# Splitting a channel transform by even and odd samples, with its sums on GpSimd, in a fused attention and spectral-filter kernel

## The chip, the cores and the metric

One core of one Trainium2 chip runs the whole program. The metric is the device time of one execution in microseconds (us), as the median of several executions. Engine names are those of the profile: PE is TensorE, DVE is VectorE, ACT is ScalarE, POOL is GpSimd and SP is SyncE, which starts most of the DMAs.

## What is computed

```
x: (1, 2048, 448) bf16      16 heads of 28 channels
g = sigmoid((x * gate_w).sum(-1))
a = softmax(q k^T * 28**-0.5) v @ wo            q, k, v = x @ wqkv
b = irfft2(rfft2(x) * (w_r + 1j * w_i))         over the 2048 rows and the 448 channels
out = g * a + (1 - g) * b
```

All inputs and the output are bf16.

## The kernel before

**Attention.** The 16 heads stand in 4 groups of 4, a head in each strip of 32 partitions. The queries are cut into 4 chunks of 512 and the keys into 16 tiles of 128. That makes 16 pairs of a group and a chunk, taken one after the other, with 16 key tiles each: 256 blocks, where a block is the scores of 4 heads, 128 keys and 512 queries. A block goes one of two ways.

- On the ACT way, two heads are one step: two matmuls write a two-bank PSUM tile (`psA` and `psB` in turn), and one exponential of 1024 columns writes two slots of `ring`, a ring of 28 slots in SBUF. Four matmuls per block then add `vw` times `ring` into the PSUM bank `pvb`.
- On the DVE way, an exponential is approximated. One matmul per head (in the plan: `dunit`) writes a single PSUM bank (`bg`), and one DVE clamp (line 991, 512 columns) makes a 16-bit pattern in a tile `pd` from it. Three `int64_add` on POOL (line 1001) make three shifted copies, each into another of the 9 `pd` tiles, and four times four matmuls with differently scaled values `vd` add all four into `pvb`.

The list `ND` says how many of the 16 key tiles of each pair go the DVE way. Its sum is 73, so 183 blocks, or 366 exponentials, go to ACT.

**The spectral part**, called the background, is done by matmuls with constant matrices, spread between the attention work. `fwd` transforms the channels of one of 16 token tiles: four chunks of 128, 128, 128 and 65 input channels against `Bd`, 450 output columns each (225 cosines and 225 sines), copied to `X1`. `fwd2` multiplies by `A`, is copied to `Ab`, and a DMA spreads it over `xtok`. `mid`, for 16 values of g, multiplies by `CS` (450, 225 and 225 columns), forms two products with the weights `Wg`, subtracts and adds these into `Z` on DVE, and multiplies `Z` by `CS` again (450, 225, 225). `inv` collects rows by a DMA into `V2`, multiplies by `A` and scales by the gate into `zt`. `out_tile` and `last_tile` add four matmuls of `zt` with `Binv` (448 columns) to four of the attention's result with the padded `wo`, and scale by the gate into the output.

**The order** of everything is fixed when the program is written. Each operation is put on a list, and a long packed number table, `TABLE`, says in which order the list is emitted and which PSUM bank each item of the background gets. Each engine then works through its own instructions in that order and waits at each for the semaphores that it needs. An engine that waits holds back all that stands behind it.

**GpSimd's code.** Before an instruction of another kind, the built program of this kernel holds a row `ISA` without a tile on POOL, which puts another library of code into GpSimd. `int64_add` stands in one library and `tensor_tensor` in another; memsets, copies and casts need neither. In the order below, `ISA pd<-pd` is an `int64_add`, and a bare `ISA` is such a change of library. The program before has one, ahead of its first `int64_add`.

Of the kernel before, what the change touches and what calls it, by code (L numbers as in the profile page):

```python
# [13 lines left out]
BF16 = mybir.dt.bfloat16  # L14
# [8 lines left out]
F2 = 2 * F  # L23
NT, J, P = 16, 8, 128
FS, FN = (0, 112), 113
# [6 lines left out]
NPD, DKT = 9, 5  # L32
FILL0 = 60000
DUE_P = 4.0
TABLE = (
    "eNoN1oNyHloUQOF9tI//NGmjKqlt27Zt27Zt27Zt27Zt+95nWDPfLA1VAIBALAiFMGgAbSAcIiASPMSGOBAX4kF8iAID0dABEkBCSASJIQkk"
    "hWSggIKEFMAgAAhpIQTSgICaYKEGdIRsUB1SQUpIDtUgHaSHypAFUoOD7JADMkEGyAnBkBEyQ1YoBjEhBlSEXFAcSkApKA1BkB9KQm7IA4td"
    "GegNVaEcVIKy0ALyQj4oDF2gAMQk5aEg1IEKUAiKwBIXi4SSp1AUnkEYCScRpAdEktjkObyAl/AKXsMbiENyYC6MS+KRtxCfRJGcGE0SkIQk"
    "EXkHK2AlrILVsAbWQmKyDtZDT0hCJsBEmASTIQ/egSmwAWpDbtwId+Ee3IdNsBm2wFbYBtthB0yD6ZAXH8AMmAmzYDbMgbkwDx5CQ9jmdkJd"
    "mA8cFkAt2AULYREshkewBJZCE3gM+bAARrvd0BSewDJoBvlxDyyHvbAP3kNLSEoK4gf4CI1hP3SFA/AJPkM3KIKF8CDUhx1uKrSFwpiMJCeH"  # L40
    "oDmE6S9QFA9DCnIEjkJKUgyPwVcI1cXxG0wnM0gqMhBmkuNQCltDCUxNTkBJ7AxVSTUyi6Qh1UlprEHSklbQCU5CGUxH0pOyWJNkIBlJJlIO"
    "T8FpOANn4RychwtwEcrjbFIBs5Ih0B4yk2wkO8lBcpJc5DvkJpfgMuQhFTEvScAqYT6y012Bq5CfJGTXYLO7DgVIQVKIVMYbcBOykFtwG6pg"
    "YVKElCFVsSgpS4qRavgDfkJx8guSsepYAyN1claO1MTy5DdUILUwWtfGcB2b1cHYOg4bTerBH6iL9bAXJGIVyRiSmI0l3aE+jiOLXBLWAIEQ"
    "QgkjDXE84aQRCIJEEkU0aYTtIIIZ8g8sScoi2V9wxJPGGCBRLiULIk0wBqlEgklc3RTj62YYxkJICZJUN8d6rgVWJqVJfVeFtMSSpIFL58JZ"
    "K0zFGrrWmN41cnFZCtYGM7h4LLnO6NpiatYOM7lolky3x4Q6DUvPOmBCV4rUIolcYtcRM7BOGJ+lZUlcOtYZE+kumJEldVG6K8bR3bAwy8Qi"
    "dGLdA7tjEVacRbFcLIlOoXthT8zBEujemJul1CVYPJ2TZWF5WCqdl2VmfbAe6Yv1STbWD1Pr7KwBaUj6YyNSlBVjAzCrzqIHYkE2CAdjMZeV"
    "FXfZdCE2BEu42iSNHoql2DCsQwqwzDqHHo4lXSVWkpVyI7AuyalHYhFdhlVm5Vg+VpblZ6MwrS7N8uvRmFuPwfIsl07mxmJ1Ng6TuxRuPKZ0"
    "FdgEzKcL6YpsIg6CSZjKZdDpdTVWg2XXRfVknIKNSV3WjOXVefRULKanYQFdlU3Heqwzqc1mYBfSlczEOmwWdiNldEfWnczGOTgXm7PCuqCu"
    "yWqxediJldLNyXxsQRZgCV1aN2ELsSmrwhZhS9KKLMYl2IK1JvVZS1ZOl9QNWW63FNuyZdiOLcfiuqxegeV1PpdOr8T8rhHL41ZhLd2YFXAZ"
    "9Wos6Aq5NdiZdWFtWAW9FnuS+nod9mC9SD29HjfgUteEZNIbsQHrySrq3qSS3oR9yGasrWvoLdjMbcW+pClp7rZhe9bCdWD9SEO9HZuRlm4H"  # L50
    "9mOtXFPdn3VjO7GOHsx2YWvWWFfVNfVu3IN92BDWQu/F5ro768v2YWXdi/VmbUk7sh8P4EjWnoxiHchBbKlHQ0cylB3Cuno8tGKHsZw7gsNY"
    "XjecjWDlXQV3FHuQiu4YjmOdSCXXSY9lx7GBPoFDSRN9EgeyUziBTWSt9Wkcz7rqRrqLHkZSuzTuDJ7DtC6bG07O4giS3Y0kg1gOl9OdxwuY"
    "y61gK1l73ZVNJAPYJVzGLuJy1k5fxklkFWtDruBksppNIcPgKo5m1XQzPZWMYTPZNWylr2M3PYlNYTewg57FJrOp7Cb2J7ewmruNHXUbPYHM"
    "Z2NgALmDbfVdnM6quxlsAbuHS9hSVsPdx866pnuA3fVisoQsJcvIQ5zNlpNa7hH20EP1AD2NDNOD9BMcRR7jXDaHbWVVtGdj9Rj9FLexZ7ib"
    "bHF7yF6yj9wjz/E+eUAekmnsEZlD9pMD5CB5TJ6Qp+QQ6amfkcPkCHlOjpJjZAh5QQaRZe44mccC7AQ5SU6RV3iavMCXOFAvZCP1XDKPrCKL"
    "yGoyn6wga8hL8oqsJevIa1xPXpMNZCPZRHrpN6S6foNvyWayhWwl28hb3E52kJ3kHS4gi9l69o5M0EP0B9zMNrD3uIsMJMP1YP0Rt7A17BOu"
    "Y3tYZfcZp+sqbrT+govYATZO72UT9VdcyxaSwWQj+4bj3Cj9Hfvpg2y828T66Ml6gvuBp9lJdortZL/wDPuJQWy8HqEnuml6kvuN8/Qf3MeG"
    "ub84S//DXWw/286Gu91shAOZ2fUBIrO4wo7KHWyKzuqYPM4m6SLuBBvpRjkuhSzqrrC5+iqbqlHeZVJeYDP0RXaYHWFztJKz9T12iGlpZHxa"
    "2pVxvbWVR1kULetmaierOi9DWDQ9xubrleQsS0ADMiYLku1cQrpAx5DnWXtX29VxwfI+6+AesMEQIju6mPIS6+TW6FhyhV6pr7FQeYacJefI"
    "eRIm++rL7AK5SC6RyyRc3mbX2Tl2hVwl18gtdoddJzfITRIhb5HbJFLeIf3cKn2XxJY7dRy5UH8ii3R/956s13Flf/2KLdOvWTy51T1kA9xA"  # L60
    "FyUXuvhyg37Etuho2c19IAnkGzbIbdPLXUK53a3VS3UM9pEkki9Yd/eEvWQ3WA+XWPZ0SWRSeVC/Zb3cOv2ZJZPP2HO2Wm/VyWVd94WlkE/Z"
    "V7ZDT3Mp5WM23X1jN9kflkru0qnlDPeXpZGMz3Scz3KbdDqZVn5k79lm3dnt1enlUOjiMshP7DvbqD+wo3qJ/sEyykzyH9un37HMcrsG3tVl"
    "kYT/ZPt1Y5dVZpOGU75bW75HZ5f94Bc7pGOxHNLxnDKUHdCtXRP3m3mueC55TB/WuWWAa55HtnFBvK37TI7ovPK4jsklzye/kK8kv0ReQJ7Q"
    "sXgkD+EXdGx+TX8j30koLygLyWAexhO423q0Kywv6cR8jDupi8gRcEcXlVf1KZ2Ep+DFZAx+RV/UxWVKHs4juOAlZFM32I11l3VJGZ+Xkj9I"
    "PP5AP9ZD3GJdWkbxm7qMTMOf67IyLf9J4vKhrpyM5tf1L5KAl5cVZEL+myzXt3RFWUkm4ql4al5ZxuFJ+Sv9h1SR6fhf8lCf0VXlI93bpefV"
    "ZFZ+Qz/R1eU/0sfVkNl5X3dPJ+P3dU2ZmdeSL/RdnZzn4Nl4Jl5bznNZeB0529WVz/R8N8fVk6d1Ab7AFeSTXX2Zkc91b3QDOcXl5G/1WZ2Y"
    "NpS5eBKalE51yWgjmZxm4E1kEZ6bN5aF+GtdmL/U5zTQpzoPbyrz8WayKM/Pm0tC32lK3+vyvARvIRmtwFvKFe6DXulaSU5XudZyl1vtdjtB"
    "i/M17oduI/PytpKbdrIkF6a9LMX3uBAak8aiofSX3uv2uQ6ykwyjH/Unfdt1lP90BD2vI2kxHpvGoZ3lXx2XdpFlOTPlODVrXVfZTZbmSCUd"
    "Cftdd9lDluHrXGOu6EnXhGtqaE9ZhfeSv3Vvud590xtcH/lTV+Vf9UanjaV95QF32vWTm1xFXp834I7+0f3lKBgga/DK/K7zNIYJMwOlNDV5"
# [78 lines left out]
def fft_consts():  # L148
# [1291 lines left out]
```

## Time and profile before

| | |
|---|---|
| median of 3 runs | 384.12 us (384.02 to 384.2) |
| profiled execution | 384.64 us; its span, first to last instruction, 382.8 us |
| granted TensorE clock | 0.999 |
| PE, DVE, ACT, POOL busy, share of the span | 98%, 87%, 90%, 65% |
| exponentials, clamps, int64_adds | 366, 292, 219 |

The page gives the busy time of each engine, the costliest groups of instructions, and the chain of work that ended last. Lines are those of the kernel before. All matmuls are issued by one helper and so share line 426; tiles tell them apart. Spans on POOL are rough by the profiler's own word.

### The profile page before, as it was taken

What the parts mean: (1) busy time and instruction counts of PE and PEld (TensorE: products, weight loads), DVE (VectorE), ACT (ScalarE), POOL (GpSimd) and SP (SyncE); (2) the same over time, 40 slices, a digit from 0 to 9 for tenths busy, and PEclk for the clock granted to TensorE, in tenths of its full rate; (3) what the DMA queues carried; (4) which work ended last, traced back from release to release, by engine and by line L of the source; (5) the groups of instructions that cost most, each with busy time, mean ns of one, the idle gap of its engine ahead of it and who ended that gap; (6) DMA issues with size and microseconds to landing.
All of it is one profiled execution on the core that took longest, in us unless ns stands there. A gap on an engine that the chain in (4) does not pass through costs nothing.

```text
span 382.8 us, 12650 instructions
## 1 busy us (share of the span) xinstructions
PE 375.9 (98%) x5140; PEld 140.7 (37%) x5141; DVE 333.4 (87%) x620; ACT 346.3 (90%) x381; POOL 247.3 (65%) x276
## 2 busy tenths in 40 slices
PE   8999999999999999999999999999999999999996
PEld 5643322233423222334434434333333333333444
DVE  1778977889899999999999999999999998878623
ACT  2699999999999999998996899999999999998861
POOL 5753874475764988647575594988769656564810
PEclk9999999999999999999999999999999999999999
DMA  8421010001112232222220132221323131122111
GB/s 228 101 58 52 4 33 2 21 25 21 22 40 48 70 130 61 53 44 71 48 65 10 30 70 47 76 57 23 82 51 82 53 97 44 46 64 64 48 57 63
DMA packets 31158, 21.68 MB, mean 57 GB/s; under 512 B 16260, under 2 KB 28796, under 8 KB 31100
## 3 DMA queue, kind: packets, MB, share of 16 engines
q1 hardware_dynamic: 29708, 20.41, 20.7%
q8 instruction: 40, 0.66, 0.7%
q10 hardware_dynamic: 1392, 0.46, 0.5%
q14 instruction: 18, 0.15, 0.1%
HBM read 14.97 MB, written 1.96 MB: 44 GB/s over the span
## 4 chain that ended last, share of the span: by engine, by line
PE 77%; DVE 9%; ACT 4%; DMA 3%; issue 2%; POOL 2%; SPq 1%; ACTq 0%; POOLq 0%; DVEq 0%
PE bg L426 31%; PE pvb L426 27%; PE psA L426 9%; PE psB L426 8%; ACT ring L1032 4%; DVE pd L991 4%; POOL pd L1001 2%; DMA X<-in_A_wqkv_dram 1%; PE bg L429 1%; DMA V<-xtok 1%; SPq L401 1%; DVE vw L864 1%; DMA Rb<-rsc 1%; DVE sq L745 1%; DMA wv<-in_gate_w_dram 1%
## 5 line engine op out<-in xcount | busy, mean ns | idle before, releaser
L1001 POOL INT64_ADD pd<-pd x219 | 224.8, 1041 | 98.8 <-DVE pd L991 23.6
L1032 ACT ACTIVATE ring<-psA 128x1024 bf16<-128x1024 f32 x183 | 192.5, 1052 | 13.0 <-PE psA L426 6.0
L991 DVE TENSOR_SCALAR pd<-bg 128x512 uint16<-128x512 f32 x292 | 190.3, 684 | 14.8 <-PE bg L426 4.7
L1032 ACT ACTIVATE ring<-psB 128x1024 bf16<-128x1024 f32 x183 | 192.5, 1052 | 5.0 <-PE psB L426 3.1
L426 PE MATMUL pvb<-pd,vd 128*32 128x512 bf16 x1168 | 102.0, 384 | 0.5 <-POOL pd L1001 0.2
L426 PE MATMUL bg<-q,k 32*128 32x512 bf16 x292 | 98.3, 383 | 0.4 <-DVE vt L877 0.3
L426 PEld LDWEIGHTS <-k 32*128 32x128 bf16 x1024 | 36.8, 91 | 117.9 <-issue 113.2
L426 PE MATMUL psA<-q,k 32*128 32x512 bf16 x366 | 71.9, 384 | 0.1
L426 PE MATMUL psB<-q,k 32*128 32x512 bf16 x366 | 71.4, 383 | 0.5 <-ACT ring L1032 0.4
L426 PE MATMUL pvb<-ring,vw 128*32 128x512 bf16 x732 | 66.7, 384 | 0.1
L426 PEld LDWEIGHTS <-vd 128*32 128x32 bf16 x1168 | 27.7, 94 | 37.3 <-issue 30.6
L426 PEld LDWEIGHTS <-vw 128*32 128x32 bf16 x732 | 17.7, 95 | 22.1 <-issue 17.4
L426 PEld LDWEIGHTS <-xT 128*128 128x128 bf16 (+3 forms) x512 | 19.3, 96 | 13.3 <-issue 11.7
L426 PE MATMUL bg<-Bd,xT 128*32 128x450 bf16 (+1 forms) x256 | 19.7, 358 | 0.0
L426 PE MATMUL bg<-xT,wpq 128*32 128x512 bf16 (+2 forms) x244 | 19.2, 382 | 0.0
L426 PE MATMUL bg<-xT,wpk 128*32 128x512 bf16 (+1 forms) x240 | 19.2, 383 | 0.0
L1343 DVE TENSOR_TENSOR t<-bg,Wg 128x450 bf16<-128x450 f32 x32 | 18.9, 618 | 0.1
L426 PE MATMUL bg<-Bd,X 113*32 113x448 bf16 x224 | 16.3, 355 | 0.0
L426 PE MATMUL bg<-wvr,xT 128*128 128x112 bf16 (+1 forms) x192 | 13.0, 213 | 0.0
L426 PEld LDWEIGHTS <-CS 128*32 128x32 bf16 x384 | 9.4, 95 | 8.7 <-issue 6.0
L1388 DVE TENSOR_TENSOR X<-bg,ogb 113x512 bf16<-113x512 f32 x16 | 10.7, 686 | 1.9 <-PE bg L426 1.7
L740 DVE TENSOR_SCALAR k<-bg 128x512 bf16<-128x512 f32 x15 | 10.3, 687 | 1.2 <-PE bg L426 1.2
(115 smaller groups left out, 297.6 us busy)
## 6 DMA issues: line engine op xcount, KB each, us to landing
Rb<-rsc SPq DMA_DIRECT2D x60, 64.0 KB
CS<-cCS SPq DMA_DIRECT2D x16, 192.0 KB
Wg<-in_B_w_i_dram SPq DMA_DIRECT2D x64, 28.1 KB
xtok<-Ab SPq DMA_DIRECT2D x16, 112.5 KB
V<-xtok SPq DMA_DIRECT2D x16, 112.5 KB
xtok<-in_A_x_dram SPq DMA_DIRECT2D x3, 448.0 KB
Wg<-in_B_w_r_dram SPq DMA_DIRECT2D x32, 28.1 KB
out_dram<-wpk SPq DMA_DIRECT2D x6, 112.0 KB
```

The source lines that it names most:

```text
L401: self.pin(e.dma_start(out=out() if callable(out) else out, in_=in_() if callable(in_) else in_))
L426: self.pin(self.nc.tensor.matmul(out, lhsT=lhsT, rhs=rhs, start=start, stop=stop, **kw))
L429: self.pin(self.nc.tensor.transpose(out=out, in_=in_, identity=self.c("ident")[0:n, 0:n]))
L740: self.pin(nc.vector.tensor_scalar(out=dst, in0=self.bgi(it), scalar1=SQ, scalar2=None, op0=ALU.mult))
L745: self.pin(nc.vector.tensor_tensor(out=sqs, in0=dst, in1=dst, op=ALU.mult))
L864: self.pin(nc.vector.tensor_tensor(out=free_dims(self.vw[g][:], [[128, nv], [32, 4], [1, DH]], 4 * b * 128), in0=src, in1=wv, op=ALU.mult))
L991: self.pin(nc.vector.tensor_scalar(out=ys[:, s, :].bitcast(U16), in0=self.bgi(it), scalar1=127 * UNITS, scalar2=0.0, op0=ALU.add, op1=ALU. ...
L1001: self.pin(nc.gpsimd.int64_add(out=fl(pds), in0=fl(ys), in1=PHASE[f] * 0x0001000100010001))
L1032: self.pin(nc.scalar.activation(out=self.ring[:, u0:u0 + len(st), :], in_=slot[:, 0:len(st), :], func=ACT.Exp, scale=LN2 / UNITS))
L1343: self.pin(nc.vector.tensor_tensor(out=out[:], in0=self.bgi(it)[:, 0:F2].rearrange("p (a f) -> p a f", a=2), in1=free_dims(Wg[:], [[F, 2], ...
L1388: self.pin(nc.vector.tensor_tensor(out=free_dims(self.zt[0:FN], [[128, 4], [1, 128]], 512 * t), in0=self.bgi(it)[0:FN, :].rearrange("p (a ...
```

## The change

**The transform.** The channels are split into even and odd ones, and only 113 frequencies are computed for each half. `fwd` has the chunks of 128, 128, 96 and 97 channels, taken with a stride of two, against 226 columns instead of 450. The other frequencies follow from sums and differences of the halves: two new `tensor_tensor` on POOL for each token tile, from `X1` into one of three tiles `Xs`, which `fwd2` now reads. On the way back, two `tensor_tensor` on POOL for each g make sums and differences of `Z` into `Zs` (the first two of the `Xs` tiles), which the second product with `CS` reads; and the four matmuls with `Binv` have 224 columns instead of 448. The output is written with a stride of two.

**PSUM.** `psA`, `psB` and three single banks become three two-bank slots, `psA`, `psB` and `psC`, and one bank `bg`. The exponentials of ACT and the clamps of DVE take the slots as the table says. Items of the background take a slot's first bank or `bg`. One clamp now covers two heads (1024 columns, 154 in place of 292).

**The share.** `ND` sums to 77, so 179 blocks (358 exponentials) are left for ACT and POOL has 231 `int64_add`. `TABLE` is new.

The diff, cut to its core:

```diff
-FS, FN = (0, 112), 113
+FS, FN = (0, 113, 226, 339), 113
+NE = 113
+CH = (128, 128, 96, 97)
+NXS = 3
-    ND = [2, 4, 5, 5] + [5] * 8 + [5, 5, 4, 3]
+    ND = [2, 5, 5, 5] + [5] * 8 + [5, 5, 5, 5]
-        self.psA = ps.tile([P, 2, 512], F32, name="psA")
-        self.psB = ps.tile([P, 2, 512], F32, name="psB")
+        self.slots = [ps.tile([P, 2, 512], F32, name="ps" + x) for x in "ABC"]
-        self.bgt = [ps.tile([P, 512], F32, name=f"bg{i}") for i in range(3)]
+        self.bgt = ps.tile([P, 512], F32, name="bg0")
+        self.Xs = [T([P, F4], BF16, f"Xs{i}") for i in range(NXS)]
+        self.Zs = self.Xs[:2]
...
     # attention(): the DVE way
-            for s in range(4):
-                it = Item()
+            for h in (0, 2):
+                it = Item(7)
...
-                    self.pin(nc.vector.tensor_scalar(out=ys[:, s, :].bitcast(U16), in0=self.bgi(it),
+                    self.pin(nc.vector.tensor_scalar(out=ys[:, h:h + 2, :].bitcast(U16), in0=self.slot(it)[:],
                                                      scalar1=127 * UNITS, scalar2=0.0, op0=ALU.add, op1=ALU.max))
...
     # out_mm()
-            self.mm4(bank, self.zt[0:FN, t, 128 * k:128 * k + 128], free_dims(self.Binv[0:FN], [[1, D]], k * D), start, stop)
+            h = D // 2 * (k in (1, 2))
+            self.mm4(bank[:, h:h + D // 2], self.zt[0:FN, t, 128 * k:128 * k + 128],
+                     free_dims(self.Binv[0:FN], [[1, D // 2]], k * (D // 2)), start, stop)
...
     # background(): fwd
-                    self.mm4(self.bgi(it)[:, 0:F2], self.xT[t // 4][0:n, c, 128 * (t % 4):128 * (t % 4) + 128],
+                    h = 2 * NE * (c % 2)
+                    self.mm4(self.bgi(it)[:, h:h + 2 * NE], self.xT[t // 4][0:n, c, 128 * (t % 4):128 * (t % 4) + 128],
                              self.Bd[0:n, c, :], c == 0, c == 3)
...
+            def lo():
+                self.pin(nc.gpsimd.tensor_tensor(out=free_dims(xs[:], [[F, 2], [1, NE]]), in0=free_dims(b, [[NE, 2], [1, NE]]),
+                                                 in1=free_dims(b, [[NE, 2], [1, NE]], 2 * NE), op=ALU.add))
+
+            def hi():
+                self.pin(nc.gpsimd.tensor_tensor(out=free_dims(xs[:], [[F, 2], [-1, NE - 1]], F - 1),
+                                                 in0=free_dims(b, [[3 * NE, 2], [1, NE - 1]]),
+                                                 in1=free_dims(b, [[-NE, 2], [1, NE - 1]], 2 * NE), op=ALU.subtract))
+            x1.append([self.pool(.6, f, [e, xr[t % NXS]], k) for f in (lo, hi)])
...
     # background(): mid
+            def zc(dif, Z=Z, zs=zs):
+                self.pin(nc.gpsimd.tensor_tensor(
+                    out=zs[:, 2 * NE * dif:2 * NE * dif + 2 * NE].rearrange("p (a f) -> p a f", a=2), in0=Z[:, :, 0:NE],
+                    in1=free_dims(Z[:], [[F, 2], [-1, NE]], F - 1), op=ALU.subtract if dif else ALU.add))
+            zc2 = [self.pool(.6, lambda d=d, zc=zc: zc(d), [z1, z2, pr[i]], k) for d in range(2)]
```

On POOL, where the forward transform begins, the program before has `int64_add` after `int64_add` (line 1001); `pd` with a number is one of the nine tiles:

```order
L1001 ISA pd_112<-pd_109 128x1024
L1001 ISA pd_111<-pd_109 128x1024
L1001 ISA pd_110<-pd_109 128x1024
L1001 ISA pd_114<-pd_113 128x1024
L1001 ISA pd_107<-pd_113 128x1024
```

The changed program has there, with line 1006 for the `int64_add` and lines 1300 and 1304 for the sums and differences of `fwd`:

```order
L1006 ISA pd_106<-pd_114 128x1024
L1304 ISA
L1304 TENSOR_TENSOR Xs_139<-X_130 128x2x112
L1300 TENSOR_TENSOR Xs_139<-X_130 128x2x113
L1006 ISA
L1006 ISA pd_107<-pd_113 128x1024
L1006 ISA pd_114<-pd_113 128x1024
```

The row `L1304 ISA` puts the library of `tensor_tensor` in place, the row `L1006 ISA` that of `int64_add`. The program has 93 such rows where it had one; 92 of them change from one of the two libraries to the other. Twelve `int64_add` stand ahead of the first `tensor_tensor`, 159 between the first and the last, and 60 behind the last.

On POOL again, in `mid` (line 1378 is `zc`), two differences are wrapped each by itself:

```order
L1378 ISA
L1378 TENSOR_TENSOR Xs_138<-Z_149 128x226
L1006 ISA
L1006 ISA pd_110<-pd_108 128x1024
L1378 ISA
L1378 TENSOR_TENSOR Xs_138<-Z_149 128x226
L1006 ISA
L1006 ISA pd_108<-pd_107 128x1024
```

Between two parts of one g, the library goes to that of `int64_add` and back for a single `int64_add`; nothing of this stood there before.

On PE, `fwd2` read `X` in the program before, behind the matmuls of a DVE block (`vd` with `pd`):

```order
L426 MATMUL pvb<-pd_110,vd_116 32x512
L426 LDWEIGHTS A
L426 MATMUL bg_65<-X_131,A 32x450
L426 LDWEIGHTS A
L426 MATMUL bg_65<-X_131,A 32x450
```

In the changed program it reads `Xs`, which POOL writes, and scores of both ways stand around it, two to a slot:

```order
L428 MATMUL psA<-q_83,k_87 128x512
L428 LDWEIGHTS k_87
L428 MATMUL psA<-q_83,k_87 128x512
L428 LDWEIGHTS k_87
L428 MATMUL psC<-q_83,k_87 128x512
L428 LDWEIGHTS k_87
L428 MATMUL psC<-q_83,k_87 128x512
...
L428 MATMUL pvb<-pd_113,vd_115 32x512
L428 LDWEIGHTS A
L428 MATMUL bg_65<-Xs_139,A 32x450
```

So PE, which waited in `fwd2` for a DVE copy alone, now also waits there for two POOL instructions and what stands ahead of them on POOL.

More of the change, by code (lines that the diff above doesn't have):

```diff
@@ L41 @@
[L41 to L45, printed above, removed]
@@ L579, in prologue @@
             b1 = (lambda i1=i1: self.bgi(i1)) if wi else (lambda: self.pv[:])
-            b2 = (self.psB if wi else self.psA)[:, 0, :]
+            i2 = Item()
+            b2 = lambda i2=i2: self.bgi(i2)
             first = {}
@@ L669, in weights, with slot @@
             self.wod.append(ds)
+    def slot(self, item):
+        return self.slots[item.bank]
     def bgi(self, item, dt=F32):
-        t = self.bgt[item.bank][:]
+        t = self.slots[item.bank][:, 0, :] if item.bank < 3 else self.bgt[:]
         return t if dt == F32 else t.bitcast(dt)
@@ L1013, in attention @@
         for i, st in enumerate(self.steps):
-            slot = self.psA if i % 2 == 0 else self.psB
-            deps = [exps[i - 2]] if i >= 2 else []
+            it, deps = Item(7), []
             for (n, kt, s) in st:
@@ L1225, in last_tile @@
         i = t - 12
-        it = Item() if i > 1 else None
-        bank = lambda: (self.psA[:, 0, :] if i == 0 else self.psB[:, 0, :] if i == 1 else self.bgi(it))[:, 0:D]
-        ops = [self.lastexp[i]] if i < 2 else []
+        it = Item()
+        bank = lambda: self.bgi(it)[:, 0:D]
+        ops = []
         for k in range(8):
@@ L1238, in last_tile @@
         if t % 2:
-            e = self.act(0.6, lambda: self.pin(nc.scalar.activation(out=fin, in_=bank(), func=ACT.Copy,
+            e = self.act(0.6, lambda: self.pin(nc.scalar.activation(out=free_dims(fin, [[1, 2], [2, D // 2]]), in_=self.runs(bank()), func=ACT.Copy,
                                                                     scale=self.glog[:, t:t + 1])),
@@ L1367, in background, with b3 @@
+            def b3(it2=it2, CS=CS, zs=zs):
+                self.mm4(free_dims(self.bgi(it2), *half(1)), CS[:, 5, :], free_dims(zs[:], *half(0)), False, True)
+            for fn, nn in ((b1, 452), (b2, 226), (b3, 226)):
+                ops2.append(self.pe(nn, fn, zc2 + dl[:1] + ops2[-1:], k, mode="col", acq=it2 if not ops2 else None))
+            pr[i] = ops2[-1]
             vev.append(self.dve(.54, lambda it2=it2, g=g: self.pin(nc.vector.tensor_copy(
-                out=self.UT[:, g, 0:F2], in_=self.bgi(it2)[:, 0:F2])), [ops2[-1], ops[-1]], k, free=it2))
+                out=self.UT[:, g, 0:F4], in_=self.bgi(it2)[:, 0:F4])), [ops2[-1], ops[-1]], k, free=it2))
```

367 lines of the change are left out of this document (186 added, 181 removed).

## The prediction

> **What bounds the kernel now.** I read the page first: busy shares, the chain that ended last, and the costliest groups.
>
> ```profile
> PE 375.9 (98%) x5140; PEld 140.7 (37%) x5141; DVE 333.4 (87%) x620; ACT 346.3 (90%) x381; POOL 247.3 (65%) x276
> PE 77%; DVE 9%; ACT 4%; DMA 3%; issue 2%; POOL 2%; SPq 1%; ACTq 0%; POOLq 0%; DVEq 0%
> L1001 POOL INT64_ADD pd<-pd x219 | 224.8, 1041 | 98.8 <-DVE pd L991 23.6
> L1032 ACT ACTIVATE ring<-psA 128x1024 bf16<-128x1024 f32 x183 | 192.5, 1052 | 13.0 <-PE psA L426 6.0
> L991 DVE TENSOR_SCALAR pd<-bg 128x512 uint16<-128x512 f32 x292 | 190.3, 684 | 14.8 <-PE bg L426 4.7
> ```
>
> PE has hardly a gap and carries three quarters of the chain. ACT stands idle for 13.0 us before the exponentials of one of its tiles. POOL has room: 98.8 us of idle time before its adds. The table of stages says where that balance holds; in each stage the columns are PE, PEld, DVE, ACT and POOL busy.
>
> ```profile
> 30.00:130.00 100.00, 99.96 (x1334) 31.81 (x1331) 88.92 (x163) 98.34 (x110) 61.86 (x68) 1.00 0.11 28
> 130.00:230.00 100.00, 99.77 (x1418) 36.68 (x1415) 99.39 (x190) 92.72 (x101) 71.64 (x73) 1.00 0.23 57
> 230.00:330.00 100.00, 99.18 (x1274) 34.77 (x1274) 95.81 (x180) 99.45 (x109) 74.14 (x74) 1.00 0.26 63
> ```
>
> From 30 to 330 us PE is full, with ACT beside it in the first and third stage and DVE in the second. POOL is never full. So a change pays here only if it relieves PE, ACT and DVE together, and it may load POOL with about a quarter more, not with a multiple.
>
> **PE, ACT and DVE.** Their rows, from the timelines of ACT, DVE and PE, the chain in order of time, and the groups kept apart by shape:
>
> ```profile
> 292.43 1.08 ACT L1032 ACTIVATE ring<-psA 128x1024 bf16<-128x1024 f32 x1
> ...
> 302.46 1.14 ACT L1032 ACTIVATE ring<-psB 128x1024 bf16<-128x1024 f32 x1
> 43.16 3.29 DVE L991 TENSOR_SCALAR pd<-bg 128x512 uint16<-128x512 f32 x5
> L877 DVE TENSOR_TENSOR vt<-bg,w 128x112 f32<-128x112 f32 x4 | 1.1, 270 | 0.0
> 45.30 0.76 PE pvb L426 x12
> 82.10 0.98 PE pvb L426 x16
> 201.03 0.39 PE L426 MATMUL psA<-q,k 32*128 32x512 bf16 x2
> 201.34 0.39 PE L426 MATMUL psB<-q,k 32*128 32x512 bf16 x2
> L426 PE MATMUL bg<-Bd,xT 128*32 128x450 bf16 x192 | 15.3, 358 | 0.0
> L426 PE MATMUL bg<-xtok,CS 128*32 128x225 bf16 x128 | 7.0, 262 | 0.0
> ```
>
> ACT: twelve exponentials start between 292.43 and 302.46 us, eleven distances of 0.91 us. Eight fewer save 8 x 0.91 = 7.3 us.
>
> DVE: five clamps in 3.29 us are (3.29 - 0.68) / 4 = 0.65 us each. From 112 columns (270 ns) to 512 (684 ns) a column costs 1.035 ns, so a clamp of 1024 columns takes 684 + 530 = 1214 ns, some 1.18 us behind another. 292 x 0.65 = 190 us become 154 x 1.18 = 182 us: 8 us less, although DVE takes four blocks more.
>
> PE: four matmuls of 512 columns cost 0.98 - 0.76 = 0.22 us. A set of score matmuls that run together costs 0.31 us (201.03 to 201.34). Two heads in one slot look like half the score sets, but a single head of the DVE way already ran beside a pair of the ACT way; counting sets that can run together in the order, I find 368 before and 374 now, 1.9 us more. The DVE blocks add 16 fours with `vd` and the ACT blocks lose 4: 12 x 0.22 = 2.6 us more. 64 fours of `fwd` and 64 of `Binv` go from about 450 columns to 225, 0.358 - 0.262 = 0.096 us each: 12.3 us less. In sum PE has 7.8 us less.
>
> So all three lose 7 to 8 us. With POOL out of the way the new end would be 384.6 - 7.5 = 377 us. Against it stands that ACT had two slots to itself and now shares three with DVE and the background; I price that at 0 to the 18 us by which ACT's waits before the exponentials would double (13.0 us on one tile, 5 on the other).
>
> The other edits I take at nothing. The first and last chunks are cut differently, and the strided reads and writes have as many elements. Padding and loads have the same count. They lie beside the first 30 us, in which a load from DRAM sets the start either way; without that cover they cost a few tenths.
>
> **POOL.** Here lies the weight. The adds and plain operations:
>
> ```profile
> 238.44 9.20 POOL L1001 INT64_ADD pd<-pd  x9 [1.98 <-DVE Z L1350]
> L525 POOL COPY wpq<-X 128x336 bf16<-128x336 bf16 x3 | 1.4, 464 | 1.6 <-DVE sq L745 1.6
> L528 POOL COPY wpq<-X 64x112 bf16<-64x112 bf16 x3 | 0.8, 275 | 4.7 <-DVE sq L745 4.6
> 34.42 1.04 POOL L1001 INT64_ADD pd<-pd  x1 [0.54 <-DVE pd L991]
> 37.79 3.07 POOL L1001 INT64_ADD pd<-pd  x3 [2.33 <-DVE vd L886]
> 41.60 2.05 POOL L1001 INT64_ADD pd<-pd  x2 [0.74 <-DVE sq L745]
> 44.03 3.19 POOL L1001 INT64_ADD pd<-pd  x3 [0.38 <-DVE pd L991]
> 50.24 7.24 POOL L1001 INT64_ADD pd<-pd  x7 [3.01 <-DVE rr L1167]
> ```
>
> Nine adds in 9.20 us are 1.02 us each, so twelve more cost 12 us. The 64 `tensor_tensor` have about 226 elements. Two copies give (464 - 275) / (336 - 112) = 0.84 ns an element and so 0.37 us for 226; a second operand at most doubles that to 0.74. I take the middle, 0.55 us, 35 us in all. POOL would have 247 + 12 + 35 = 294 us of work, under 80% of 377 us, and would still not bound.
>
> But between the two kinds of instruction the program changes GpSimd's library 92 times, and each change stands on POOL's own queue. The trace of before holds one, in the view of line 1001:
>
> ```profile
> L1001 POOL INT64_ADD pd<-pd x219: 1035/1039/1323, 34.4 to 364.1; - x110
> L1001 POOLq MODIFY_POOL_CONFIG  x2: 4/4/4, 33.8 to 33.9; - x2
> 33.63 0.25 POOL L815 CAST vw<-w 128x16 bf16<-128x16 f32 x1
> ```
>
> The change is two instructions of 4 ns at 33.8 us, and the first add starts at 34.42. So this one cost 0.54 us at most, and that time is put down to a clamp. I don't take this as the price. The program has only this one library to ask for, nothing takes it out again, and the execution before left it in place: the row can show a change that had nothing to change. In the changed program each of the 92 finds the other library.
>
> What does fetching code and putting it into an engine cost? No row shows it for POOL. The nearest are a table put into ACT, a load from DRAM at the start of the chain, and a spread between partitions of SBUF late in it:
>
> ```profile
> L570 ACT ACT_TABLE_LOAD x1 | 1.3, 1283 | 3.6 <-DMA cst<-ccst 3.6
> 1.83 4.82 DMA X<-in_A_wqkv_dram
> 345.29 3.79 DMA V<-xtok
> ```
>
> A fetch and then a fill, 4.82 + 1.28 = 6.1 us, is my estimate for one change. The low end for a real fetch is one transfer, 3.79 us; the high end is two in series, 4.82 + 3.79 = 8.6 us. Below these stand the 1.28 us of a table alone and, at the bottom, nothing.
>
> With such a price POOL becomes the bound and runs through from the first change to the last. The twelfth add of before ends near 53 us (nine to 47.2, three of the next seven), and the change puts twelve ahead of its first `tensor_tensor`. Then follow 159 adds, 162 us; 64 `tensor_tensor`, 35 us; and 92 changes, 92 x 6.1 = 561 us. Behind the last one, what remains is the end of the program as now:
>
> ```profile
> L426 PE MATMUL bg<-Z,CS x192: 258/261/364, 166.4 to 300.6; 128*32 128x225 bf16 x128, 128*32 128x450 bf16 x64
> ```
>
> The last product with `Z` starts at 300.6 of 382.8 us, 82 us from the end. In the order 185 score matmuls stand behind it, and 234 behind its like in the change: 82 x 234 / 185 = 104, taken as 100 us. The sum is 53 + 162 + 35 + 561 + 100 = 911 us of span. The profiled execution was 384.64 us against a span of 382.8 us, and 0.5 us above the median; with that the time is 912 us.
>
> POOL's idle time gives no cover: the 98.8 us are used up by the first sixteen changes. Who waits is clear from the order. Behind a change stand the adds of the next blocks, for which PE waits in `pvb`; PE takes its queue in order, so the scores behind that come late, and ACT and DVE with them.
>
> On this point the Trainium skill, GPSIMD Engine Reference, section 2.1 (Instruction dispatch), says that the first call into a freshly loaded library pays about 6 us of code loading, 5.95 us measured from MODIFY_POOL_CONFIG on, with no visible instruction for it. By that figure, as an estimate, the changes are 92 x 5.95 = 547 us and the time is 898 us. The 0.54 us above do not agree with it, unless the library was not freshly loaded there.
>
> **The rivals.** (1) A change of library costs almost nothing even when it really changes, as the row at 33.8 us looks. POOL's sum without changes is 53 + 162 + 35 + 100 = 350 us, under the 377 us of the other engines, so these decide: 377 us, faster. It turns at (382.8 - 350) / 92 = 0.36 us a change; at the full 0.54 us POOL's sum is 400 us. For it speaks the one row there is, against it that it can show a library already in place. Chance 0.12.
>
> (2) A change is a short fill like ACT's table, 1.28 us, with the fetch hidden: 350 + 118 = 468, or 470 us, slower. Against it speaks that nothing announces the next library ahead of its turn on the queue. Chance 0.06.
>
> (3) Changes are free, but the shared slots hold ACT up: 377 + 18 = 395 us, slower. The second and third stage have ACT or DVE full, which speaks for it; that POOL's price must be nil as well speaks against. Chance 0.02.
>
> **How the numbers follow.** The forecast, a real reload at each change, has the other 0.80, since no other reading makes a use of two libraries in turn free. Its low end, 3.79 us a change, gives 350 + 349 = 699, or 700 us; its high end, 8.6 us, gives 350 + 792 = 1142, or 1145 us. The range 700 to 1145 holds this case and leaves out the other three, 0.20. A measurement of this kernel can tell about 0.2%. Faster by over that is rival 1 at 0.12, and 0.01 for ending within it; slower is 0.87.
>
> **What would show it.** In the changed profile POOL should have idle gaps of about 6 us before the first instruction behind each pair of MODIFY_POOL_CONFIG, put down to nothing that ended then, and PE, ACT and DVE should be busy for well under half of the span, with PE waiting for POOL before `pvb` and before `fwd2`. Until about 53 us the two kernels should run alike, and in the last 100 us again. Gaps below 1 us at the changes would make the forecast wrong; then ACT's waits before its exponentials and the 1.18 us of a clamp are what to look at.

## The result and the profile after

| | before | after |
|---|---|---|
| median | 384.16 us (384.02 to 384.85) | 983.96 us (980.47 to 991.73) |
| profiled execution, its span | 384.64, 382.8 us | 980.47, 978.6 us |
| granted TensorE clock | 0.999 | 0.662 |

The changed kernel takes 2.563 times as long (interval 2.548 to 2.579). (One execution each of `e6_before_excursions`, the profiled one, and of `e9_psum_operand` below was disturbed; the times given are those of the others, and only idle times are read from the profile of `e6_before_excursions`.) First the page of the changed kernel: busy times, the slices for PE, POOL and the granted clock, and the costliest groups.

```profile
PE 472.5 (48%) x5188; PEld 160.2 (16%) x5189; DVE 345.5 (35%) x478; ACT 353.0 (36%) x373; POOL 295.4 (30%) x352
PE   9954423521343250323624282563255362538998
POOL 6641211311113131111513141331224141316773
PEclk9977557555565555555765776665576575557999
L1006 POOL INT64_ADD pd<-pd x231 | 237.2, 1037 | 325.2 <-issue 261.0
L428 PE MATMUL pvb<-pd,vd 128*32 128x512 bf16 x1232 | 141.3, 486 | 289.4 <-POOL pd L1006 288.3
L1378 POOL TENSOR_TENSOR Xs<-Z 128x226 bf16<-128x226 bf16 x32 | 18.3, 580 | 150.2 <-issue 136.0
L1300 POOL TENSOR_TENSOR Xs<-X 128x226 bf16<-128x226 bf16 x16 | 8.9, 554 | 93.9 <-issue 79.3
L1304 POOL TENSOR_TENSOR Xs<-X 128x224 bf16<-128x224 bf16 x16 | 8.9, 555 | 85.9 <-issue 85.8
```

No engine is busy for half of the span, POOL least of all. Yet POOL's four groups are idle for 655 us ahead of their instructions, and 562 us of that are `issue`: nothing that the profile shows ended then. PE in turn idles for 288 us before `pvb`, released by the adds. PE's slices show the normal program at the two ends and a thinned one between.

POOL's timeline from 40 us on is where the pattern can be read; the bracket is the idle time before a row.

```profile
44.99 5.10 POOL L1006 INT64_ADD pd<-pd  x5 [1.05 <-PE bg L428]
56.76 0.55 POOL L1304 TENSOR_TENSOR Xs<-X 128x224 bf16<-128x224 bf16 x1 [6.67 <-issue]
57.39 0.56 POOL L1300 TENSOR_TENSOR Xs<-X 128x226 bf16<-128x226 bf16 x1
63.76 2.05 POOL L1006 INT64_ADD pd<-pd  x2 [5.80 <-issue]
66.00 1.04 POOL L1006 INT64_ADD pd<-pd  x1 [0.19 <-PE pvb L428]
67.91 1.04 POOL L1006 INT64_ADD pd<-pd  x1 [0.87 <-DVE pd L996]
...
83.83 0.55 POOL L1300 TENSOR_TENSOR Xs<-X 128x226 bf16<-128x226 bf16 x1 [7.01 <-issue]
90.36 1.03 POOL L1006 INT64_ADD pd<-pd  x1 [5.98 <-issue]
98.53 0.56 POOL L1304 TENSOR_TENSOR Xs<-X 128x224 bf16<-128x224 bf16 x1 [7.14 <-issue]
```

A `tensor_tensor` comes about 7 us behind the add before it, an add about 6 us behind the `tensor_tensor`. A second `tensor_tensor` right behind the first (57.39) has no gap. The view of waits adds them up (total, times, longest):

```profile
PE pvb L428 <- POOL pd L1006: 288.3, 39, 26.1
POOL pd L1006 <- issue: 261.0, 46, 6.3
ACT ring L1036 <- PE psA L428: 234.0, 52, 22.1
POOL Xs L1378 <- issue: 136.0, 19, 7.6
PE bg L428 <- POOL Xs L1378: 128.7, 15, 21.6
POOL Xs L1304 <- issue: 85.8, 12, 7.5
POOL Xs L1300 <- issue: 79.3, 11, 7.5
```

42 gaps before sums are 301.1 us, 7.2 each; the other four changes that way are put down to other releasers. The 46 gaps before adds are not the 46 changes back: three of them, of 0.3 to 2.3 us, stand at no change, and three changes back are put down to other releasers. Taken change by change from POOL's timeline, the 46 gaps on the way out are 329.8 us, 7.2 each (6.7 to 7.6), and the 46 on the way back 274.3 us, 6.0 each (5.7 to 6.3): 604.1 us in all, 6.57 a change. ACT and DVE wait for PE, and PE for POOL.

### The profile page after: what moved, and what is told of

Same layout as the page of the kernel before. It is cut to its first block, busy times and chain, and to the rows that moved or that the text cites. A ratio compares the mean times of both kernels' runs of the same rounds, so it can differ in the third digit from the quotient of the medians.

```text
span 978.6 us, 12927 instructions
## 1 busy us (share of the span) xinstructions
PE 472.5 (48%) x5188; PEld 160.2 (16%) x5189; DVE 345.5 (35%) x478; ACT 353.0 (36%) x373; POOL 295.4 (30%) x352
## 2 busy tenths in 40 slices
DMA packets 31160, 21.25 MB, mean 22 GB/s; under 512 B 16260, under 2 KB 29052, under 8 KB 31100
## 5 line engine op out<-in xcount | busy, mean ns | idle before, releaser
L1006 POOL INT64_ADD pd<-pd x231 | 237.2, 1037 | 325.2 <-issue 261.0
L428 PE MATMUL pvb<-pd,vd 128*32 128x512 bf16 x1232 | 141.3, 486 | 289.4 <-POOL pd L1006 288.3
L1036 ACT ACTIVATE ring<-psA 128x1024 bf16<-128x1024 f32 x139 | 143.0, 1029 | 266.2 <-PE psA L428 204.2
L1036 ACT ACTIVATE ring<-psB 128x1024 bf16<-128x1024 f32 x124 | 127.7, 1030 | 187.5 <-PE psB L428 123.9
L996 DVE TENSOR_SCALAR pd<-psC 128x1024 uint16<-128x1024 f32 x73 | 89.3, 1223 | 195.9 <-PE psC L428 121.4
L1036 ACT ACTIVATE ring<-psC 128x1024 bf16<-128x1024 f32 x95 | 97.8, 1030 | 127.3 <-PE psC L428 107.0
L996 DVE TENSOR_SCALAR pd<-psB 128x1024 uint16<-128x1024 f32 x47 | 57.4, 1221 | 88.0 <-PE psB L428 49.5
L428 PE MATMUL psC<-q,k 32*128 32x512 bf16 x336 | 79.5, 468 | 0.2 <-ACT ring L1036 0.2
L428 PE MATMUL bg<-Xs,CS 128*32 128x452 bf16 (+1 forms) x180 | 15.8, 445 | 128.7 <-POOL Xs L1378 128.7
L1378 POOL TENSOR_TENSOR Xs<-Z 128x226 bf16<-128x226 bf16 x32 | 18.3, 580 | 150.2 <-issue 136.0
L996 DVE TENSOR_SCALAR pd<-psA 128x1024 uint16<-128x1024 f32 x34 | 41.6, 1223 | 16.5 <-PE psA L428 14.5
L1304 POOL TENSOR_TENSOR Xs<-X 128x224 bf16<-128x224 bf16 x16 | 8.9, 555 | 85.9 <-issue 85.8
```

What stands on the lines that cost most here:

```text
L428: self.pin(self.nc.tensor.matmul(out, lhsT=lhsT, rhs=rhs, start=start, stop=stop, **kw))
L996: self.pin(nc.vector.tensor_scalar(out=ys[:, h:h + 2, :].bitcast(U16), in0=self.slot(it)[:], scalar1=127 * UNITS, scalar2=0.0, op0=ALU.add ...
L1006: self.pin(nc.gpsimd.int64_add(out=fl(pds), in0=fl(ys), in1=PHASE[f] * 0x0001000100010001))
L1036: self.pin(nc.scalar.activation(out=self.ring[:, u0:u0 + len(st), :], in_=self.slot(it)[:, 0:len(st), :], func=ACT.Exp, scale=LN2 / UNITS))
L1304: self.pin(nc.gpsimd.tensor_tensor(out=free_dims(xs[:], [[F, 2], [-1, NE - 1]], F - 1), in0=free_dims(b, [[3 * NE, 2], [1, NE - 1]]), in1= ...
L1378: self.pin(nc.gpsimd.tensor_tensor(out=zs[:, 2 * NE * dif:2 * NE * dif + 2 * NE].rearrange("p (a f) -> p a f", a=2), in0=Z[:, :, 0:NE], in ...
```

## The experiments

**Theory:** the time goes into changes of library, some 6.5 us each, with nothing that covers them. **Rivals:** the sums themselves, or the detour through `Xs` and `Zs`, are slow; the new slots or the split cost the time; the low granted clock of PE is a cause of its own.

**Sums without a change of library.** `e1_dve_sums` puts all 64 sums on VectorE.

```diff
-    self.pin(nc.gpsimd.tensor_tensor(   # lo, hi, zc
+    self.pin(nc.vector.tensor_tensor(
```

> The changed kernel with all 64 sums and differences on VectorE instead of GpSimd, in the same places of the order; nothing else differs, and the order holds one change of GpSimd's library instead of 93. Theory R (each change of library costs GpSimd's queue some 6.5 us: 92 of them are 598 of the 979 us): the span falls to 377 us and the 64 sums on VectorE at some 0.2 us each, 13 us, can show in part: 377 to 392 us, granted clock back at 0.99. Rival C (the low granted TensorE clock, 0.66, is what stretches the program, for a reason of its own): the clock and with it the time stay where they are, above 600 us. Rival P (the detour of the data through GpSimd, PE waiting for VectorE, then GpSimd, in queues that keep their order): falls as with R, since the detour is gone.

`e2_pool_copies` leaves them on GpSimd, in the same places of its queue, but as copies of the first operand; the second operand is left out.

```diff
-    self.pin(nc.gpsimd.tensor_tensor(out=..., in0=..., in1=..., op=...))   # lo, hi, zc
+    self.pin(nc.gpsimd.tensor_copy(out=..., in_=...))
```

> The changed kernel with each of the 64 sums on GpSimd replaced by a copy of its first operand, on GpSimd, at the same place, with the same output tile; the second operand is left out, so part of the transform is not computed. Copies need no library: one change instead of 93. Theory R: 377 to 395 us. Rival P (the detour through GpSimd's queue): all waits for GpSimd are kept, so the time stays far above, over 600 us. Rival C: over 600 us at a granted clock near 0.66.

Measured: 407.1 us with VectorE (ratio 1.061, 1.055 to 1.067) and 381.86 us with the copies (0.993, 0.991 to 0.996). The busy times of the kernel with copies, and two rows of its copies in the view of the tile `Xs`:

```profile
PE 371.7 (98%) x5188; PEld 149.9 (39%) x5189; DVE 334.7 (88%) x478; ACT 342.3 (90%) x373; POOL 279.3 (73%) x352
L1376 POOL COPY Xs<-Z x32: 370/374/484, 161.8 to 286.9; 128x226 bf16<-128x226 bf16 x32
L1303 POOL COPY Xs<-X x16: 369/372/487, 50.6 to 142.1; 128x224 bf16<-128x224 bf16 x16
```

The same detour over POOL and the same queue, 352 instructions in both, cost nothing when no library changes. So the 602.1 us between the two kernels are 6.54 us for each of the 92 changes, where the gaps above are 6.57. The 64 sums also outlast their copies by 0.2 us each, 13 us in all. Gaps and sums together are thus 15 us more than the difference; by this subtraction some 15 of the 604 us fell into time in which POOL stood idle anyway. With VectorE the time missed the 377 to 392 us that the theory had; its rows, with the least, median and longest duration, say why:

```profile
L1304 DVE TENSOR_TENSOR Xs<-X x16: 206/418/1103, 53.5 to 158.5; 128x224 bf16<-128x224 bf16 x16
L1300 DVE TENSOR_TENSOR Xs<-X x16: 250/475/1077, 54.4 to 161.6; 128x226 bf16<-128x226 bf16 x16
L1378 DVE TENSOR_TENSOR Xs<-Z x32: 264/280/1111, 175.2 to 309.9; 128x226 bf16<-128x226 bf16 x32
```

One shape takes 0.21 or 1.10 us. The timelines of POOL and DVE show what the long ones wait for:

```profile
53.18 2.06 POOL L1006 INT64_ADD pd<-pd  x2 [1.78 <-DVE pd L996]
53.52 0.82 DVE L1304 TENSOR_TENSOR Xs<-X 128x224 bf16<-128x224 bf16 x1
54.38 0.99 DVE L1300 TENSOR_TENSOR Xs<-X 128x226 bf16<-128x226 bf16 x1
```

The two adds end at 54.21 and 55.24 us, the two sums 0.13 us behind them, at 54.34 and 55.37. Of the 64 sums in this trace, 33 start while an add runs, and they end 0.13 us behind the end of that add (0.2 us in the two that start in its last 0.07 us); the other 31 take 0.21 to 0.28 us. So a sum that starts beside an add on POOL waits for its end. DVE's busy time rises to 359.6 us.

**Fewer changes.** `e3_joined` puts the two sums of a token tile, and of a g, together at the place of the later one: 62 changes. `e4_mid_dve` puts only the sums of `mid` on VectorE: 50 changes.

```diff
-            x1.append([self.pool(.6, f, [e, xr[t % NXS]], k) for f in (lo, hi)])
+            x1.append([self.pool(.6, f, [e, xr[t % NXS]], k) for f in self.joined(lo, hi)])   # e3; zc alike
...
-                self.pin(nc.gpsimd.tensor_tensor(   # e4, in zc alone
+                self.pin(nc.vector.tensor_tensor(
```

> The changed kernel with the two GpSimd instructions of each token tile, and of each g, put together at the place of the later one. All 64 sums stay on GpSimd; the changes of library fall from 92 to 62. Theory R: 984 - 30 x 6.5 = 789 us, 760 to 820. Rival P: the same sums in the same queue, some of them later: 984 us give or take 20. Rival C: no relation to the number of changes, 984 us.

> The changed kernel with the 32 sums of the middle part on VectorE and the 32 of the forward transform still on GpSimd: 50 changes of library instead of 92. Theory R: 984 - 42 x 6.5 = 711 us, and a few us for VectorE: 690 to 740. In the first half of the program the gaps of 6 to 7 us stay, in the second there are none and the clock is back. Rival P: half of the sums gone, (984 + 377) / 2 = 680 us. Rival C: the clock stays low all through.

Measured: 793.72 us (ratio 2.066, 2.060 to 2.072) and 717.4 us (1.868, 1.858 to 1.877), both as the price per change has it. Joined, (793.72 - 381.86) / 62 = 6.64 us a change, with all 64 sums in place: the count of changes sets the time, not the count of sums. In `e4_mid_dve` the last change ends at 472 us; the granted clock is 0.58 from 50 to 470 us, while the changes last, and 0.97 from there on.

**Is it the reload, or the exchange?** `e5_same_library` is the kernel before with the library that is already in place asked for again ahead of every tenth add, 21 times. `e6_before_excursions` is the kernel before with a `tensor_tensor` of two columns there, whose result nobody reads: 42 changes.

```diff
+                def g2(g1=g1):
+                    self.nadd = getattr(self, "nadd", 0) + 1
+                    if self.nadd % 10 == 0:
+                        self.pin(nc.gpsimd.load_library(LIB))   # e5
+                        self.pin(nc.gpsimd.tensor_tensor(out=self.tiny[:, 0:2], in0=self.tiny[:, 2:4], in1=self.tiny[:, 4:6], op=ALU.add))   # e6, instead
+                    g1()
-                o = self.pool(1.0, g1, p1s, fdue[f] - 2.0, name="dexp")
+                o = self.pool(1.0, g2, p1s, fdue[f] - 2.0, name="dexp")
```

> The kernel before, with a reload of the library that is in place already put ahead of every tenth int64_add: 21 more changes in name, none of which changes anything. If a reload costs only where it brings in another library (the reading of the row at 33.8 us in the prediction): gaps under 1 us and 384 to 386 us. Rival (every reload costs its 6 us, and the one of before only looked cheap): 21 x 6 = 126 us on GpSimd's queue, of which its 98.8 us of idle time can take part: 400 to 500 us.

> The kernel before, with a tensor_tensor on two columns of a scratch tile put on GpSimd ahead of every tenth int64_add. No data of the kernel goes through it and no engine waits for its result; it makes 42 changes of library. Theory R (7.1 us towards the one library, 5.9 us back, on GpSimd's queue): 42 x 6.5 = 273 us more in that queue, less what its 98.8 us of idle time takes up: 384 + 273 - 99 = 558 up to 657 us, and a low granted clock where PE waits. Rival P (it is the detour of data through GpSimd that costs): no detour here, 384 to 395 us.

Measured: 384.17 us with the reloads (ratio 0.9992, 0.9982 to 1.0001). The first of them falls into this stretch of POOL's timeline, and the row with the reloads is behind it:

```profile
44.20 3.19 POOL L1002 INT64_ADD pd<-pd  x3 [0.38 <-DVE pd L992]
50.41 7.24 POOL L1002 INT64_ADD pd<-pd  x7 [3.02 <-DVE rr L1174]
...
L1007 POOLq MODIFY_POOL_CONFIG  x42: 10/11/13, 47.3 to 349.9; - x42
```

Without them the seven adds began at 50.24. A reload of a library in place is two instructions of 11 ns and no gap, which is what the one change of the kernel before, at 33.8 us, had shown. The changed kernel's own first change, at 29.6 us, is as cheap, with 0.15 us between a memset and an add, as it would be if the last change of the execution before had left the library of `int64_add` in place. The excursions took 668.02 us against 384.58, (668.02 - 384.58) / 42 = 6.75 us each, above the 558 to 657 that I expected. POOL's timeline there, and the row of its adds:

```profile
43.87 3.19 POOL L1005 INT64_ADD pd<-pd  x3 [0.38 <-DVE pd L995]
54.09 0.18 POOL L1010 TENSOR_TENSOR tiny<-tiny 128x2 bf16<-128x2 bf16 x1 [7.04 <-issue]
60.22 6.12 POOL L1005 INT64_ADD pd<-pd  x6 [5.94 <-issue]
68.15 1.04 POOL L1005 INT64_ADD pd<-pd  x1 [1.81 <-DVE pd L995]
71.35 2.06 POOL L1005 INT64_ADD pd<-pd  x2 [2.16 <-PE pvb L427]
...
L1005 POOL INT64_ADD pd<-pd x219 | 225.0, 1038 | 237.1 <-issue 126.1 <-DVE pd L995 32.1 <-DVE sq L749 12.9
```

7.04 us out and 5.94 back, for a sum of 0.18 us that no one waits for. I had let POOL's 98.8 us of idle time absorb part of that. They absorb none: without the gaps of the changes the adds still have 237.1 - 126.1 = 111.0 us of idle time ahead of them. Once the adds are back, POOL waits for a clamp (1.81) and for PE (2.16) again, since PE, which waits for the adds for 228.0 us in all, and DVE behind it stood still meanwhile.

**What the rest of the change is worth.** `e7_full_columns` keeps the slots, the wide clamps and the 77 blocks, but takes the split away (450 and 448 columns, no sums). `e8_no_detour` keeps the halved columns and leaves the sums out altogether, so its products read `X1` and `Z` as they are. Both read `Z` in place, from four buffers where there were two.

```diff
-            x1.append([self.pool(.6, f, [e, xr[t % NXS]], k) for f in (lo, hi)])
+            x1.append([self.pool(.6, lambda: None, [e, xr[t % NXS]], k) for _ in range(2)])   # both; zc alike
...
-                    h = 2 * NE * (c % 2)                                   # e7 alone
-                    self.mm4(self.bgi(it)[:, h:h + 2 * NE], self.xT[t // 4][0:n, c, ...],
+                    self.mm4(self.bgi(it)[:, 0:F2], self.xT[t // 4][0:n, c, ...],
                              self.Bd[0:n, c, :], c == 0, c == 3)
```

> The changed kernel without the split: 450 columns again in the forward transform and 448 with Binv, no sums, the rest of the change (slots, clamps of 1024 columns, 77 blocks, table) kept. Expected by the terms of the prediction: PE's 12.3 us come back on top of what the next kernel gives, so that kernel plus 12 us if PE bounds it, 389 to 394 us. Rival (ACT bounds, PE's saving is not on the path): within 3 us of the next kernel.

> The changed kernel with the halved columns, and with the sums left out altogether: neither sums nor copies stand on GpSimd, the products read X1 and Z directly, so part of the transform is not computed. Expected by the prediction's 377 us for changes that cost nothing: 376 to 379 us, if the 64 copies in GpSimd's queue are what kept the kernel with copies at 382 us. Rival (the copies are covered; the saving on PE, ACT and DVE was put too high): 381 to 383 us.

Measured: 391.22 us without the split (ratio 1.018, 1.016 to 1.020), 381.28 us without the sums (0.992, 0.989 to 0.994). The busy times, of the first and then of the second:

```profile
PE 382.2 (98%) x5188; PEld 148.4 (38%) x5189; DVE 335.4 (86%) x478; ACT 344.0 (88%) x373; POOL 259.2 (67%) x288
```

```profile
PE 370.2 (98%) x5188; PEld 149.1 (39%) x5189; DVE 334.8 (88%) x478; ACT 342.0 (90%) x373; POOL 259.3 (68%) x288
```

The split takes 12.0 us off PE's busy time and 9.9 us off the time. All that is not the split (slots, wide clamps, 77 blocks, the new table and the new cut of the channels) adds 6.3 us to PE's 375.9 and 6.6 us to the time: the time follows PE in both kernels. Even with sums that cost nothing the change would have brought 3.3 us. The copies of `e2_pool_copies` (381.86) come within 0.6 us of that.

**Is the low clock a cause?** `e10_busy_pe` is the changed kernel with 24 sets of matmuls that add zero put on PE behind each sum, where `pvb` is open.

```diff
+            def busy(f):
+                f()
+                for _ in range(24):
+                    self.filler(0, 256)
-            x1.append([self.pool(.6, f, [e, xr[t % NXS]], k) for f in (lo, hi)])
+            x1.append([self.pool(.6, lambda f=f: busy(f), [e, xr[t % NXS]], k) for f in (lo, hi)])   # zc alike
```

> The changed kernel with 24 sets of matmuls that add zeros put on PE behind each sum of GpSimd, wherever the accumulation in pvb is open: PE has work while it would wait for GpSimd. Theory R (GpSimd's queue sets the pace; the low granted clock of 0.66 follows from PE's waiting and costs little): the clock rises, the time stays within 3% of 984 us, 955 to 1010. Rival C (the low clock is what stretches the program): with the clock up the time falls by a fifth or more, under 800 us.

Measured: 980.36 us (ratio 2.550, 2.544 to 2.557). Two stages of the changed kernel and then the first of them in this one, columns as in the prediction:

```profile
150.00:300.00 150.00, 51.07 (x486) 15.05 (x475) 34.19 (x46) 36.40 (x38) 26.92 (x33) 0.56 0.04 9
...
500.00:700.00 200.00, 89.55 (x916) 29.85 (x915) 69.10 (x103) 60.26 (x62) 52.11 (x60) 0.62 0.08 20
```

```profile
150.00:300.00 150.00, 82.03 (x1556) 45.99 (x1555) 35.11 (x48) 37.85 (x39) 27.76 (x34) 0.71 0.04 10
```

From 150 to 300 us PE does three times the matmuls at a clock of 0.71 in place of 0.56, and the other engines get as much done as before. A clock raised by a quarter takes nothing off the time: the low clock follows from the waiting and is no cause of its own here.

**A version that pays?** `e9_psum_operand` does the forward sums on VectorE straight from PSUM, with only the odd half copied to SBUF first, and those of `mid` on VectorE. `e11_before_split` is the kernel before with the forward split alone, its sums done in that way.

```diff
+                self.pin(nc.vector.tensor_copy(out=self.Qh[t % 2][:], in_=b[:, 2 * NE:F4]))          # e11; e9 alike
+                self.pin(nc.vector.tensor_tensor(out=free_dims(xs, [[F + NE - 1, 2], [1, NE]]), in0=p, in1=h, op=ALU.add))
+                self.pin(nc.vector.tensor_tensor(out=free_dims(xs, [[NE, 2], [-1, NE]], F - 1), in0=p, in1=h, op=ALU.subtract))
-            x1.append(self.dve(.54, lambda: self.pin(nc.vector.tensor_copy(
-                out=self.X1[:, t, 0:F2], in_=self.bgi(it)[:, 0:F2])), ops[-1:] + pads, k, free=it))
+            x1.append(self.dve(.54, fe, ops[-1:] + pads, k, free=it))
```

> The changed kernel with all sums on VectorE, those of the forward transform taken from PSUM: only the odd half is copied to SBUF, and each sum has one operand in PSUM and one in SBUF. If the 407 us of the kernel with sums on VectorE come from VectorE waiting beside GpSimd's adds where both operands are in SBUF (single instructions of up to 1.1 us where the shortest took 0.2), the forward half of it goes: 390 to 399 us. Rival (it is the plain number of instructions on a full VectorE): 404 to 410 us, since there are more of them now.

> The kernel before, with the split of the forward transform alone: even and odd channels, 226 columns, the sums on VectorE with one operand in PSUM, two for each token tile; the way back, the PSUM tiles, the clamps and the 73 blocks as before. The two runs with and without the split differ by 9.9 us for both ways, so PE gains 5 us; VectorE does one copy of 226 columns and two sums of 226 instead of a copy of 450, some 0.4 us more for each of 16 tiles, 6.7 us, between 35 and 170 us, where it is busy for 89 to 99%. PE bounds: 379 to 382 us. Rival (VectorE bounds there): 384 to 390 us.

Measured: 402.16 us (ratio 1.046, 1.042 to 1.050), between what the two theories had; and 391.54 us (1.018, 1.015 to 1.020), where I had expected a gain. The second one's sums and its first stage:

```profile
L1297 DVE TENSOR_TENSOR X<-bg,Qh x16: 393/394/395, 41.4 to 138.4; 128x226 bf16<-128x226 f32 x16
30.00:130.00 100.00, 96.30 (x1272) 32.50 (x1270) 90.42 (x182) 95.66 (x106) 57.09 (x63) 1.00 0.11 25
```

With an operand in PSUM the same 226 columns take a steady 393 to 395 ns, beside an `int64_add` or not. But three instructions of 0.38 to 0.40 us stand in DVE's queue for one copy of 0.62 us, and in this stage PE falls from 99.96 to 96.30 us of 100. Over the whole program the products with `Bd` and `Binv` do fill 5.8 us less of PE's time (31.91 after 37.75 us), but the scores fill 6.0 us more (146.35 after 140.38). So PE's busy time is 378.0 us after 375.9, and its idle time 12.9 us after 6.9. Counted by their starts, with 0.2 us to a set, the scores run in 382 sets, where there were 368, so fewer of them run side by side. That later clamps break up the sets is the likely reason; no run shows it apart. I found no version that beats the kernel before.

## Why the prediction was right

**The sum, term by term.** The forecast of 912 us stands against 983.96, and the terms of its 911 us of span against 978.6:

| term | predicted | measured |
|---|---|---|
| up to the first `tensor_tensor` | 53 us | 50.0, where its change begins |
| 92 changes | 561, 6.1 each | 604, 6.6 each (7.2 out, 6.0 back) |
| 159 adds | 162 | 162 |
| 64 `tensor_tensor` | 35 | 36 |
| POOL waiting for others, and eight small operations, between them | 0 | 30, what is left over |
| behind the last sum (measured: behind the last change) | 100 | 96 |

Two rows of the changed kernel carry the first, the fourth and the last term. The last sum starts at 876.5 us, and with the change behind it the adds are back at 882.9 of 978.6 us.

```profile
L1304 POOLq MODIFY_POOL_CONFIG  x24: 1/1/13, 50.0 to 441.3; - x24
L1378 POOL TENSOR_TENSOR Xs<-Z x32: 579/580/582, 495.1 to 876.5; 128x226 bf16<-128x226 bf16 x32
```

**The mechanism** was the one named: POOL's queue runs through, PE waits for it in `pvb` and `fwd2`, and ACT and DVE behind PE. ACT (36%) and DVE (35%) are busy for well under half of the span, as foretold; PE, at 48%, only just. `e2_pool_copies` shows that it is the changes and nothing else on POOL; `e3_joined` and `e6_before_excursions` that it goes by their count, in either kernel.

**The price** of 6.1 us, from a load from DRAM and a table put into ACT, was a proxy. It came within 8% of the 6.57 us, and that is luck: what a change spends its time on is in no row. The fetch from DRAM that the proxy pictures is not seen, for the profile counts 31158 DMA packets before and 31160 with 92 changes more. The figure of 5.95 us in the Trainium skill, GPSIMD Engine Reference, section 2.1 (Instruction dispatch), agrees with the way back in the timeline (5.80 and 5.98 us); the way out (6.67 to 7.14) is up to 1.2 us longer. That the figure is for a freshly loaded library alone agrees with `e5_same_library`.

**Not taking the 0.54 us** at 33.8 us as the price decided the size: at that price POOL's sum was 400 us, slower too, but by 4%. The reason given, a library already in place, was only argued then; `e5_same_library` shows it.

**No idle of POOL as cover** was right, but for a poorer reason than the true one. I let it be used up by the first sixteen changes, as if it were there to be used. `e6_before_excursions` shows that it covers none there, because PE and DVE stop as well. In the changed kernel it covers some 15 of the 604 us by the subtraction above, and 27 of the 30 us left over in the table are waits of the same kind, which the forecast had put at nothing.

**PE, ACT and DVE.** Of the 7.8 us that PE was to lose, the split had 12.3, measured 12.0; the score sets and the `vd` fours were put at 4.5 us more, and all that is not the split came to 6.3 (the scores had been put at 374 sets after 368, 1.9 us more; counted by their starts, with 0.2 us to a set, they ran in 368 before and 385 in `e7_full_columns`, which at 0.31 us are 5.3 us). In `e8_no_detour` PE is busy for 5.7 us less than before and ACT for 4.3 (342.0 after 346.3), but DVE for 1.4 more (334.8 after 333.4), where all three were to lose 7 to 8 us. A clamp of 1024 columns was to take 1214 ns and took 1223, but the 154 of them were put at 182 us and fill 188.0 in `e8_no_detour`. So the case without a price per change was not 377 but about 381 us, and rival 1 would have been less than half the gain that I gave it. Rival 3, slots that hold ACT up, is not needed for it: of the 6.9 us by which the span of `e7_full_columns` is longer (389.7 us), 6.3 are PE's own work, and only 0.6 us more of PE's time is idle.

## What to carry to other kernels

An instruction moved to GpSimd is priced with the library that it needs: list the changes of library in POOL's order, and count each at 6 to 7 us of a queue that stands still. Group the instructions of one library, or keep to copies and casts, which need none; an engine's idle share is no cover when the others wait for it. And a row that shows such a step for next to nothing may be showing the one case in which there was nothing to do.

## What the runs showed of the hardware

- A change of GpSimd's library costs 7.2 us towards that of `tensor_tensor` and 6.0 us back to that of `int64_add`; asking for the one in place costs nothing measurable (ratio 0.9992).
- The granted clock of TensorE falls to 0.56 and 0.62 in stages in which PE is busy for 34% and 45% of the time. Over the whole of the changed kernel (granted clock 0.662) the matmuls of `pvb` with `vd` take 486 ns on average, where the row of the kernel before has

```profile
L426 PE MATMUL pvb<-pd,vd 128*32 128x512 bf16 x1168 | 102.0, 384 | 0.5 <-POOL pd L1001 0.2
```

  The Trainium skill, TensorE: Matmul & The Clock Gate, Part 1, says that the throttled state is the default and activity lifts it; the filled PE of `e10_busy_pe`, at 0.71 where it was 0.56, agrees.
- A `tensor_tensor` of 224 or 226 columns on VectorE with both operands in SBUF took 0.21 to 0.28 us where it started beside no `int64_add` of GpSimd. Where it started while one ran it took up to 1.11 us and ended 0.13 to 0.2 us behind the end of that add. With one operand in PSUM it took a steady 0.39 us either way. What the two engines share is in no row.
